# A fused attention and SwiGLU kernel on one core: one hand-kept order and engine table replaced by another

## The chip, the cores and the metric

The kernel runs on 1 core of one Trainium2 chip. The metric is the device time of one execution in microseconds (us). The kernel before took 261.92 us (median of 3 runs, 260.77 to 262.48). The engines of the core are TensorE (PE), VectorE (DVE), ScalarE (ACT), GpSimd (POOL) and SyncE (SP), which issues nearly all transfers.

## The reference

Attention over 4 batches, 8 heads, 768 positions of 64 values, then a feed-forward block on the 3072 tokens of 512 values:

```python
scores = q @ k.T / sqrt(64)
# heads 0, 2, 6: causal; the other heads: causal, and only the first 4 keys or the last 64
a = softmax(where(mask, scores, -1e9));  x = (a @ v) -> [3072, 512]
g = x @ w_gate                           # 512 -> 1536
out = (g * sigmoid(g) * (x @ w_val)) @ w_out   # 1536 -> 512
```

All inputs and outputs are float32. The kernel computes in float16 with float32 accumulation.

## The kernel before

The kernel first describes its work as 1073 named steps. Each has the engines that may run it, in a fixed order. Two long strings then decide everything that matters here. `ORDER` lists the steps, two characters each in base 62, in the order in which they are emitted, so it is each engine's order too. `WAYS` holds one digit per step and picks its engine. Numbers from 3700 up in `ORDER` are fillers: that many matmuls of the identity, whose result nobody reads.

```python
class Plan:
    FILL = 3700
    def order(self):
        n = len(self.tasks)
        numbers = [DIGITS.index(ORDER[2*i]) * 62 + DIGITS.index(ORDER[2*i+1])
                   for i in range(len(ORDER) // 2)]
        ...                             # a check of both strings, cut
        for t, w in zip(self.tasks, WAYS):
            t.way = t.ways[int(w)]          # engine of this step
        return numbers
...
for number in P.order():
    if number < P.FILL: P.tasks[number].run()
    else:               warm(number - P.FILL)   # fillers

def copy(task, dst, src):                        # all casts, copies, evictions (L175, L177)
    if task.way == "ACT": nc.scalar.copy(out=dst, in_=src)
    else:                 ENG[task.way].tensor_copy(out=dst, in_=src)
```

The steps with a choice that the argument touches are these (cut):

```python
P.add(f"cx{n}.{m}.{j}", ["ACT","DVE","POOL"], castv ...)      # V block n, float32 to float16, into vt
P.add(f"wc {kd}{n}",    ["ACT","DVE","POOL"], wcast ...)      # weights: g gate, v value, o output
P.add(f"mask{t}.{u}",   ["DVE","POOL"],       mask ...)       # L557: e = e * m, both in SBUF
P.add(f"sk{b}.{i}", ["DVE","POOL","ACT"], sinks_k ...)        # copies of the first 4 keys
P.add(f"sv{b}.{i}", ["DVE","POOL","ACT"], sinks_v ...)        # and of their values, inside SBUF
P.add("fill3",          ["DVE","POOL"],       ...)            # zero fill of hqz
P.add(f"oe{g}.{tt}",    ["ACT","DVE"],        ...)            # eviction of an output tile, from PSUM
# only DVE:  stt1: sil = (tanh + 1) * gate      stt2: h = sil * 0.5 * value     (L780, L787)
#            rc, nm: the division after attention (L574, L586)
```

The chain of a token tile runs like this. Load (SP), cast, transpose (PE), eviction to kT/qT, scores (PE, L539), exp (ACT, L549), mask (L557), attention times values (PE, L569), division (DVE, L586), transpose (PE, L602), gate and value matmuls (PE, L770), tanh (ACT, L776), stt1 and stt2 (DVE), output matmuls (PE, L799), eviction and store. Each engine runs its steps in the order of its list, so a late step delays those behind it: in the kernel before, VectorE's mask of 61.66 us took 1.79 us, and the multiply for h behind it started at 63.38 us.

The softmax here doesn't subtract the row's maximum and nothing guards it: scores larger than these inputs give would overflow.

## Time and profile before

| | before |
|---|---|
| median time | 261.92 us |
| profiled span | 259.0 us |
| useful TensorE work (own count over the matmul records) | 235.0 us |
| fillers | 131 matmuls, 40 of them in the opening block |
| DVE / ACT / POOL busy | 178.5 / 134.1 / 86.2 us |
| granted TensorE clock | 1.00 from 5.49 us until after the last matmul |

How to read it: TensorE is the bound, and "useful" is what it cannot do without. I give every useful matmul the distance to the next one that it shows when packed back to back; the prediction lists these distances, and the two matmuls of 384 columns get 162 ns. In a stretch of the timeline, what remains after the useful work is **lost**: fillers, or waits. All comparisons below are made in lost microseconds per stretch. The profile lines of this kernel that carry the argument stand in the prediction.

### The profile page before, as it was taken

To read this page: it belongs to the slowest core of one execution; us is meant where nothing else is said; L and a number is where in the kernel's file an instruction comes from. 1 tells how busy PE (TensorE), PEld (TensorE's weight loads), DVE (VectorE), ACT (ScalarE), POOL (GpSimd) and SP (SyncE) were. 2 spreads that over 40 slices of the span, in tenths; PEclk is the share of its full clock that TensorE was granted. 3 is DMA by queue.
4 is the path that set the end of the run, shared out by engine and by line. 5 is a ranking of instruction groups with operands and counts; after the bars stand their busy time and mean duration, and the time that the engine had idled before them with its cause. 6 is when DMAs were issued, how large, how long until landed. Compare 5 with 4: busy or idle time off the path is not lost.

```text
span 259.0 us, 5044 instructions
## 1 busy us (share of the span) xinstructions
PE 248.4 (96%) x1910; PEld 142.9 (55%) x1910; DVE 178.5 (69%) x360; ACT 134.1 (52%) x210; POOL 86.2 (33%) x122
## 2 busy tenths in 40 slices
PE   7979999998998999999999999999999999999992
PEld 7967667664554645555555546555545544444440
DVE  2877999989877676684877698776656547354621
ACT  2568977776764546596565445434752403421000
POOL 7335997672352355504802652000330000000000
PEclk9999999999999999999999999999999999999999
DMA  7999999966985799999569875551012320111243
GB/s 189 292 305 316 337 314 315 337 164 158 345 246 114 194 202 231 318 223 220 113 122 240 168 138 126 104 122 23 0 41 63 67 55 3 41 39 43 53 114 81
DMA packets 80377, 42.55 MB, mean 164 GB/s; under 512 B 32736, under 2 KB 75744, under 8 KB 80352
## 3 DMA queue, kind: packets, MB, share of 16 engines
q1 hardware_dynamic: 80272, 42.09, 66.8%
q8 instruction: 15, 0.25, 0.4%
q10 hardware_dynamic: 80, 0.13, 0.2%
q14 instruction: 10, 0.08, 0.1%
HBM read 28.31 MB, written 6.29 MB: 134 GB/s over the span
## 4 chain that ended last, share of the span: by engine, by line
PE 82%; DMA 6%; DVE 5%; SPq 3%; issue 1%; ACT 1%; POOL 0%; DVEq 0%; POOLq 0%; ACTq 0%
PE gv L770 43%; PE o_ps L799 23%; PE sc L539 8%; PE av L569 5%; DMA raw<-in_q_dram 3%; SPq L309 2%; DMA raw<-in_k_dram 2%; DVE h L787 1%; DVE vt L177 1%; PE xtr L602 1%; ACT e L549 1%; DVE sil L780 1%; DVE e L557 1%; DVE xb L586 1%; PE warm L285 1%
## 5 line engine op out<-in xcount | busy, mean ns | idle before, releaser
L549 ACT ACTIVATE e<-sc 128x1024 f16<-128x1024 f32 (+4 forms) x71 | 62.1, 878 | 32.4 <-PE sc L539 31.8
L770 PE MATMUL gv<-xt,wg_sb 128*128 128x512 f16 (+1 forms) x304 | 72.7, 368 | 1.6 <-DVE h L787 1.5
L770 PE MATMUL gv<-xt,wv_sb 128*128 128x512 f16 (+1 forms) x304 | 72.3, 368 | 0.6 <-DVE sil L780 0.6
L799 PE MATMUL o_ps<-wo_sb,h 128*128 128x512 f16 x288 | 69.4, 379 | 0.0
L776 ACT ACTIVATE sig<-gv 128x512 f32<-128x512 f32 (+1 forms) x76 | 43.1, 575 | 43.8 <-PE gv L770 42.1
L780 DVE SCALAR_TENSOR_TENSOR sil<-sig,gv 128x512 f32<-128x512 f32 (+1 forms) x76 | 49.1, 654 | 21.3 <-ACT sig L776 19.9
L787 DVE SCALAR_TENSOR_TENSOR h<-sil,gv 128x512 f16<-128x512 f32 (+1 forms) x76 | 49.2, 655 | 18.8 <-PE gv L770 17.3
L770 PEld LDWEIGHTS <-wv_sb 128*128 128x128 f16 x304 | 28.9, 98 | 28.4 <-issue 1.0
L799 PEld LDWEIGHTS <-h 128*128 128x128 f16 x288 | 27.6, 98 | 30.2
L770 PEld LDWEIGHTS <-wg_sb 128*128 128x128 f16 x304 | 28.6, 98 | 28.3 <-issue 2.1
L539 PE MATMUL sc<-qT,kT 128*128 128x256 f16 (+1 forms) x276 | 37.4, 257 | 0.2 <-ACT e L549 0.2
L557 POOL TENSOR_TENSOR e<-e,m 128x1024 f16<-128x1024 f16 (+1 forms) x15 | 28.5, 1903 | 23.7 <-ACT e L549 18.2
L539 PEld LDWEIGHTS <-kT 128*128 128x128 f16 x276 | 24.5, 97 | 11.0 <-issue 0.6
L569 PEld LDWEIGHTS <-e 128*128 128x128 f16 x472 | 19.9, 97 | 8.6 <-DVE xb L586 1.3
L569 PE MATMUL av<-vt,e 128*128 128x65 f16 x472 | 22.0, 193 | 1.0 <-DVE xb L586 0.7
L175 ACT COPY o_sb<-o_ps 128x512 f32<-128x512 f32 x13 | 7.6, 584 | 29.0 <-PE o_ps L799 27.9
L586 DVE TENSOR_TENSOR xb<-av,rc 128x256 f16<-128x256 f32 x47 | 19.8, 424 | 1.6
L177 POOL CAST hq<-raw 128x1024 f16<-128x1024 f32 (+1 forms) x12 | 12.0, 1001 | 17.9 <-DMA raw<-in_k_dram 12.1
L557 DVE TENSOR_TENSOR e<-e,m 128x640 f16<-128x640 f16 (+1 forms) x23 | 15.2, 667 | 2.7 <-ACT e L549 2.6
L177 POOL CAST vt<-raw 64x512 f16<-64x512 f32 x22 | 15.4, 700 | 5.0 <-DMA raw<-in_v_dram 3.4
L177 POOL COPY vt<-vt 2x330 f16<-2x330 f16 x18 | 8.4, 464 | 22.9 <-PE av L569 22.4
L574 DVE RECIPROCAL rc<-av 128x4 f32<-128x4 f32 x48 | 8.4, 176 | 9.9 <-PE av L569 9.7
(61 smaller groups left out, 142.2 us busy)
## 6 DMA issues: line engine op xcount, KB each, us to landing
raw<-in_q_dram SPq DMA_DIRECT2D x12, 512.0 KB, 5.5
raw<-in_k_dram SPq DMA_DIRECT2D x12, 512.0 KB, 6.7
raw<-in_v_dram SPq DMA_DIRECT2D x12, 512.0 KB, 6.5
out_dram<-o_sb SPq DMA_DIRECT2D x47, 128.0 KB, 2.4
raw<-in_moe_w_gate_dram SPq DMA_DIRECT2D x6, 512.0 KB, 7.1
raw<-in_moe_w_val_dram SPq DMA_DIRECT2D x6, 512.0 KB, 7.7
raw<-in_moe_w_out_dram SPq DMA_DIRECT2D x6, 512.0 KB, 6.7
xt<-xb SPq DMA_TRANSPOSE x16, 2.5
```

The source lines that it names most:

```text
L177: ENG[task.way].tensor_copy(out=dst, in_=src)
L539: nc.tensor.matmul(sc[c // 4][:, c % 4:c % 4 + n, :], weights, moving, start=first, stop=last)
L549: nc.scalar.activation(out=e[:, 0:n], in_=whole_sc.pop((t, u))[:, 0:n], func=AF.Exp, scale=scale)
L557: ENG[task().way].tensor_tensor(out=ev, in0=ev, in1=mm, op=ALU.mult)
L569: nc.tensor.matmul(av[:, n, 0:65], ee, vv, start=(m == 0), stop=(m == len(bl) - 1))
L574: nc.vector.reciprocal(out=rc, in_=avs[t, odd][:, :, 64:65])
L586: nc.vector.tensor_tensor(out=xbs[t][:, :, odd, :], in0=av[:, :, 0:64], in1=rc.to_broadcast([128, 4, 64]), op=ALU.mult)
L770: nc.tensor.matmul(ps, wsb[:, kk, j * 128:(j + 1) * 128], xt[:, kk, c[0]:c[1]], start=(kk == 0), stop=(kk == 3))
L776: nc.scalar.activation(out=sg[g, j, c], in_=gs[g, j, c], func=AF.Tanh, scale=0.5)
L780: nc.vector.scalar_tensor_tensor(out=sl[g, j, c], in0=sg.pop((g, j, c)), scalar=1.0, op0=ALU.add, in1=gs.pop((g, j, c)), op1=ALU.mult)
L787: nc.vector.scalar_tensor_tensor(out=hs[g, j][:, c[0]:c[1]], in0=sl.pop((g, j, c)), scalar=0.5, op0=ALU.mult, in1=vs.pop((g, j, c)), op1=A ...
L799: nc.tensor.matmul(o_open[g, tt], hs[g, j][:, tt * 128:(tt + 1) * 128], wo_sb[:, j, :], start=(j == 0), stop=(j == NJ - 1))
```

## The change

The intent: keep VectorE's copies, casts and masks, whose operands lie in SBUF, apart in time from GpSimd's work, since such a step beside GpSimd's took up to 1.79 us instead of 0.67 (lines in the prediction); reorder the loads for the start; drop fillers. Nothing but the two strings changes. All 35 lines of them differ, so the diff is cut to its head.

```diff
 ORDER = (
-    "030208041L0900011Mxr1T0B1X1N1W1O1V1Uxz1Y1Z1axw1n0C2526281o0A1r1d1K1P2D272H1e1t1u2E1p0E0D2I2G2K2J"
 ...
+    "0004081L021M1T1U09011W1N1Oxy1Y1V1a1Z1Xxr1t1u031r1s0B0A25262D2G1P2H1R1S2F1p1b1d1c1Q1n1f1y1z1e0C27"
 ...
 WAYS = (
-    "000000000000000000000000000000000000000000000000000000000000002222222222022200211200210211100111"
+    "000000000000000000000000000000000000000000000000000000000000002100222222022020222210101220101110"
 ...
```

Decoded, by kind of step (before to after). In all, 115 steps change their engine; kinds whose counts change by one at most (casts and evictions of Q and K, evictions to the gate's input) are left out.

| kind | DVE | POOL | ACT |
|---|---|---|---|
| masks | 23 to 20 | 15 to 18 | |
| key sink copies (steps) | 4 to 1 | 8 to 11 | |
| value sink copies (steps) | 5 to 3 | | 2 to 4 |
| casts of V | 14 to 11 | | 12 to 15 |
| value weight casts | 1 to 0 | 5 to 4 | 1 to 3 |
| gate weight casts | | 5 to 6 | 1 to 0 |
| output weight casts | | 5 to 4 | 1 to 2 |
| output evictions | 10 to 15 | | 14 to 9 |
| zero fill of hqz | 1 to 0 | 0 to 1 | |

Loads, with x for V, g, v, o for weights, in order of issue:

```
before: q0 k0 q1 k1 x0 q2 x1 k2 g1 v1 q3 g2 k3 x2 v2 g0 g4 v0 ...
after:  q0 k0 q1 x0 k1 q2 k2 x1 g1 v1 g0 q3 x2 k3 g2 v0 g4 v2 ...
```

Fillers after the opening block of 40: 91 become 50 (18, 11, 11, 5 and 5).

More of the change, by code (lines that the diff above doesn't have):

```diff
@@ L16 @@
 ORDER = (
-    "030208041L0900011Mxr1T0B1X1N1W1O1V1Uxz1Y1Z1axw1n0C2526281o0A1r1d1K1P2D272H1e1t1u2E1p0E0D2I2G2K2J"
-    "1b2F1c0F1q1Qxv1f1s1R1S1g2V2j2W0j1i211h1j0p1v1w1x1y2C1k2p2q0H2r2A2k1z2Lxw1l2M1m292N2O2X15202P2s2B"
-    "2t2Z2axm232b162Y2x2y0k2c249Z2d2e2h2i2Q2u2v0I9j2R362S2T2U9k3Q9lxo309o9a319b053W2g9p073X9m9n9q180G"
-    "3D3E3Y06229y9z3R3A9r3B9s3Z9c3M3a2w9d9t0q9u9eA02l2z2m32333b0i199f9g2o9w0m9v343c3G9x35A1A2109F3H9h"
-    "1E9i3C9G112n370o3e9K0l129H0K9L3p13389M9P9Q9I3I9S9J3f9U9R3d0J3j3k9V3FAI9W9T3t3u391B0L3T493U9N9X3J"
@@ L22 @@
-    "4F3K3w9Y2fA80n4H9OAD3S4GAJAK3L3x1H3hA9AE3NAF4A4I3i3lAN3z3V3vAS0s1FAAAL3m3g3n404JAM3o413OAGAOAPAT"
-    "420O3q3y43440t4N4q4O1IA3453PAH4K3r464LAV0M3sAU47A44WAWA54Z0r0u4a1C48AB4CA6A7AC4M4f0N4BBLAQ0v4o4y"
-    "4g4c4xARBMBN4S4T4b4p4EBOBP4dBaBb4v4wBf4l4QBQBc0QBgBh4PBRB6Bd0PBS4D4eB7Be4RB152530z0w4UB24X0x5WB8"
-    "B94VBA4rBBBC4zB3504hBT17B45556BU1J545DBD4YBiBE0RB55G4iBj5H5I0y1D4s0U1ABG4j4k4nBk4m5V5cBF14BHAX5d"
-    "AY5MAw4tBI1G4uAZ5N5X5eAz5O5fAa5P51595AAcBl570SAdAeAb585B5EAxAyB0Af5C5JAr0b5K5L5Q5RBn63Bm6B5b5g5S"
@@ L27 @@
-    "5h5TAhAiBV5ZBoBWAsAt5FAj5iAk5r0TBXBY5Y5s5j5k5UAmBJBKAn5o625a615p0XD2D35lAoAl6A5q68BZApC969D4Au5m"
-    "CACE5tAv7S5uBpBqCJ5vCBCH6i5yCFCG0V677RCI6I665wCiCK6J0WCj0h65CMCL5z6F6G7TCNAq6g6HBr0a6qCC0YCD8b6C"
-    "Cl6h64CkCm6DCnCoBsAgCpCq5n6pCr6OCY6E7PCZ6X6YCaCsCtD0Bu6R6S6TCx6oCy8d5xCzD1Bv6UBw6n6VCd6K0ZCb6L6l"
-    "6d6r7XBx6M6PCe0g6sCuByCTCU6NBzCc6u6Q6ZCf6v6W7OC0C1606a7N7VD5D66b6k6e7Q6zBt6c7W70CO6jC2Cv6xC46w6f"
-    "Cw756yC57U0d8c6m788e79CVC6CWC7C87v7B6t71CPCQ7C0f72Dy83DvDwCX730c7Y7ZDxDzE5CRCg7GE6E77HCSE0Ch7gE8"
@@ L32 @@
-    "D774E1E27h76E9EKEL7a7ED87tEM7bDR7ADS7FDUD9Dl7c7uDTDm7dDVDA7j7kDnDoDpE37iDb0e7e7mE47DDcDd7zDq81Dg"
-    "Dh7q7l7nDi8a7w8280848Z8i85DCC3Dr7o7r777pDjDk8788DD7I7JDsDEDF7KDB7L897f7x8Y8f8G8MDWDHDt8g8NDX868C"
-    "DuDY8AEAEN8BEB8P7MEFEO8hEG8QDZDI8D8EECDa8J8KEHDJDK7sEIEJ8HEDDe8FEoEEF3DfEpEq8VDMDN7yFXFYEr8O8L8R"
-    "8S8m8nDOF48TFZ8j8kEsF5FDFEFFFaFbDG8UDL8x8IEt8l938WEuFGEvFI8t94FH8r8sFcFdDPFeDQ9091EwEPEQExFJFK8p"
-    "8qFfEj8uERFgFNESEkF6F7ETEUEV8o8v988w8zFOFP92ElFLEWEXFSFQFTFM958y99FU9AEy9BEYFR96EzF1EZ8XF0979CF2"
@@ L37 @@
-    "F89D9EEaEbEcF9FAFVFBEmFWEeEfEgEnEhFCG6GkG7G8GlG9GmGAGnEdGLGMGoGpGNGsFhGQFiFjGqGrGtGRGSFkGOGPGGGH"
-    "GuGvGwFlGaFmGJGIGKGbGxFnFoFpGcGdGeG1FrFqGTG2GyFsFtGfGgG3GBFuGhGUFwFxGCGVGDGEGFG4G5FvGWFyGYGiFzG0"
-    "GXGZGjEiGzH0H1H4H5H6H9H2HAHBH3H7H8HEHFHGHCHDHHHI"
+    "0004081L021M1T1U09011W1N1Oxy1Y1V1a1Z1Xxr1t1u031r1s0B0A25262D2G1P2H1R1S2F1p1b1d1c1Q1n1f1y1z1e0C27"
+    "282I1o2E1q1g2K2Jxr2V0E2j1h0F211i1v1w1x2p2r2q2W2L222k2M1jxl2s200D2t2X1k2C292A2N1l2O2P2B1mxl2Z0j15"
+    "230p2Y2u242v2a2b162c9Z9a2d2e1K9j0i9k0H2Q2R2S2h9m0G2i0I9b2x0k36112T3Q0o9l9n9c9d2U9o052y2f9e9f3W06"
@@ new lines @@
+    "109p3X0m3A9g9q3B9h9P2m9i9Q9r30319F3Y9G3R2l9s2n3D183Z3E9y072z133G3H2w32129R9S9H3a9t3M3j3k9T331E9u"
+    "0q199I9J349v3h9z3CAD3iAE35AF0n371HA1A03b3F2o3c0J3S380L3I3J0K3V9wA23T9K9x9L9M393e9X3K9UAS3L3O3f9V"
+    "0t9W3p9N0s493P3N0l9Y0r3t3d4A9O3u4I0x3gATANAO1I2g3U3l3z4JAP1B0NAI404FAUAQ3mAVAR3n4H0M3vAW3o1C1F3w"
+    "4G3qA3AJAK3xAG3y434E3r0OA44142A84N3s444OAH4546A6A94K4LA5A74C47480vAL0R4B1D0zAMAB4W174c4dAAArAsAC"
+    "0u4MAu0yBVAt4Z4SBWAvBXAw4P4aBYBZ0w4QAzBf4q4R4TAxAy4l4f0V4o4p4w4UBiB0BgBh1ABkBjBn4V4X14BlBm4gAXBa"
@@ new lines @@
+    "1J4bBoB64D4h4yB7B84xBb5XBcBT1GAYAZAa4vBQ5253Ac0Q4eAd544zBLBRBSBUBd504Y4iBe55BGAe51Af5D565W5J5K0P"
+    "0SAbBHBI4uB14j4k5V5G5HAhAi0e4t5L66575Z584r4sAj4m5MB259B95ABM675IBNBA0UAkAm5B5c5C5d5N5EBB63B3B45Q"
+    "5RAg5O5fAn5P5S7z5e5TAoB50TAl5g5b624nAp5hBOBEBp5oBCBD5F5aBP5p5Y5UBJCYCZBF0X5rCsBKCT61645i696BCa0W"
+    "6i5j5k5sCUBqBrCVCt6A685lCv7xCuCwCOCP5mBsCR5q5uCQ5vCJ0YCW6h5y6FCKAqCS6GCXCLCxCyCzCb0aCc5t5w5z6g6q"
+    "6CD06OCq6D6IBu6J6oCnCo6U6H0b6VD1Ci0ZCj6jCpCr656pCk5xBv6n6E6R6S7NC9CABwCgBtCB6X6T6W6K5n606kClCC6L"
@@ new lines @@
+    "6Y7P7X6d6M6r6P7RCmBxByCD6NCdCe0hBzC06Z6Q0d6s6uD26v6aCf7O6b6c757vCE6e6wCF6fChCG7E7FC1CM6t6z0c7W7T"
+    "D3C2CHCIC470C5716xD46m6yCN7VE5E6E8C6E7787U797SE9D5D6Dq7A8372EA0g7BEBDrECEKDsC77C73Db7Q74ELDcDd7j"
+    "7k8bDt7lD7C8Du6l7Y7ZDW7D76EMENEODv7t7aDX7I7JDZ0fDYDa7G7H7uD8EFDwDx7g7K7LD9DADy8aDzED7b7c80DlDC7d"
+    "7hEEDm7y7qEG81827eDn8h8YC3Dg7i8iDBDDDE777f8ZEH87DF88EIEJDhDUDi848G857mDRDoDpDS8e8ADH7nDIDTDV7w8B"
+    "7MDJ8P8Q7oDeE08JDK8K8g7pDfDMDN89867r8CDGE18M8D8N7sFXE2FYE3E4FZEtEuDODP8f8V8jEv8k8E8F8L8HFaEwFbDj"
@@ L40 @@
+    "8pExFI8qDkEP8RDQ8cEQER8OFN8SFOFPFJ8m8xFQFK8T8WFD8n90FRFEFFFS8U91Ej8oESDLEkEmElEUEn8d938l8t8uFGEo"
+    "EV94Ep8I8rFHEqFTFUFVEW8s8v8yEX8wEY92F8FWErF98X8zFLFM9A9BEZFAEa95EbEsEcFc96F3Fd97Ff98EeET99Fe9CFg"
+    "9DFBFCEyEfEgF6F4EzF0F1F5EhF79EG6F2G7GpGqG8GBGsGCGrGtGDFhGEGfG1EiGgGFGhG2FiFjFkFlGLG4FmG3GQEdG5GM"
+    "GNGRGiGjGGGHFnFoFpFqGTFrFsFtGSGUGIGOGkGVGPGlFuFwGYGWGXGZG9FxGAGnGmGoGJGKFyFvGaGbFzG0GdGuGvGcGeGw"
+    "GxGzH0GyH1H2H3H4H5H6H7H8H9HAHBHCHEHDHFHGHHHI"
 )
 WAYS = (
-    "000000000000000000000000000000000000000000000000000000000000002222222222022200211200210211100111"
@@ L43 @@
-    "011000000000101000000000000000100211222010101101100000000000000000000110121220201101000000000000"
-    "100000100000000011012220220000000000000000000010000100100000000002220000110100000000000011000000"
-    "100000010002212020000000000000000002100000000000000001012121000000100000001001000001001200220000"
-    "000000000000210001001000000220020202200000000010000000020000100000000000012022110000001000000010"
-    "000000110122120100000000000000001000000000000000201020111000000100000000000100001000000000000000"
@@ L48 @@
-    "000000000000000000000000000000000000000000000000000000000000000000000000000000000000000000000000"
-    "000000000000000000000000000000000000000000000000000000000000000000000000001000000000000000000000"
-    "000000000000000000000000000000000000000000000000100001000010000100000000000000000000000000000000"
-    "000000000000000000000000000000000000000000100000000000000000000000000000000000000000000000000000"
-    "000000000000000000000000001000010000000000000000000000000000000000000000000000000000000000000000"
@@ L53 @@
-    "10000000001000000"
+    "000000000000000000000000000000000000000000000000000000000000002100222222022020222210101220101110"
+    "011000000100000000000000000001201112020210011101100000000010000000000110022022001101000001000000"
+    "110000000100000011002220220010100000000000000200000000100000000000222020000100000000000011000000"
+    "100000011000212000000001001000000002000010000000000002010202000000100000001001000021021102220000"
+    "000000000000110000000000000020022111000000000010000000012000000000000000021011200000000000000000"
@@ new lines @@
+    "000000200102221200000010010000001100010000000001102201100000000100100000000120001001000000000000"
+    "000000000000000000000000000000000000000000000000000000000000000000000000000000000000010000000001"
+    "000000000000000000000000000000000000000000000000000000000000000010000100001000010000000000000000"
+    "000000000000000000000000000000000000000000000000000001000010000100000000000000000000000000000000"
+    "000000000000000000000000000000000000000000100001000000000000000000000000000000000000000000000000"
@@ L54 @@
+    "000000000000000000000000001000000000000000000000000000000000000000000000000000000000000000000000"
+    "10000100001000000"
 )
```

## The prediction

> **What bounds the kernel now.** I began with the page's span, the busy time of each engine and the 40 slices.
>
> ```profile
> span 259.0 us, 5044 instructions
> PE 248.4 (96%) x1910; PEld 142.9 (55%) x1910; DVE 178.5 (69%) x360; ACT 134.1 (52%) x210; POOL 86.2 (33%) x122
> PE   7979999998998999999999999999999999999992
> DVE  2877999989877676684877698776656547354621
> POOL 7335997672352355504802652000330000000000
> ```
>
> TensorE (PE) is full nearly everywhere, VectorE (DVE) is close to full only from the fifth to the thirteenth slice, GpSimd (POOL) matters in the first half alone. But "96% busy" counts fillers (matmuls of the identity that are thrown away) and counts overlapping matmuls as one stretch, so it doesn't say how much could be won. For that I took the start of each of the 1910 matmul records in the trace and the distance to the next start. Back to back, that distance is 216 ns for 512 columns, 109 for 256, 56 for 128 and 30 for the 65-column ones. Counting each useful matmul at its own figure gives 62.3 us for the output projection (288 matmuls), 124.3 for gate and value (608), 28.1 for scores and masks, 13.9 for attention times values, 6.2 for transposes and 0.2 for the mask order: **235.0 us of useful TensorE work**. It is the same before and after. The first useful matmul starts at 6.17 us, the last one at 253.9 us. In between are 247.7 us, so 12.7 us are lost, and 5.1 us follow for the last eviction and store. That 12.7 us is all there is to win after the first data; a perfect order would end near 246.3 us.
>
> Then the same stretch by stretch, with the view of windows.
>
> ```profile
> 6.17:22.50 16.33, 14.95 (x228) 13.29 (x226) 13.57 (x36) 10.15 (x19) 6.47 (x8) 1.00 1.15 303
> 22.50:60.00 37.50, 36.42 (x371) 25.64 (x368) 33.98 (x80) 31.21 (x47) 28.94 (x42) 1.00 0.99 283
> 60.00:90.00 30.00, 28.44 (x232) 15.75 (x231) 23.91 (x44) 17.90 (x29) 11.06 (x14) 1.00 0.84 222
> 90.00:160.00 70.00, 69.57 (x483) 37.10 (x480) 51.61 (x98) 41.84 (x67) 30.49 (x34) 1.00 0.92 195
> 160.00:254.00 94.00, 94.00 (x567) 46.33 (x563) 52.78 (x99) 30.49 (x49) 4.55 (x4) 1.00 0.25 55
> ```
>
> The columns are the stretch, its length, then busy us and count of PE, its weight load, DVE, ACT, POOL, then clock, DMA share and GB/s. Useful work by my count is 9.8 us of the first stretch, 34.6 of the second, about 28.2, 68.7 and 93.7 of the others. So the losses are **6.5, 2.9, 1.8, 1.3 and 0.2 us**. In the first stretch 72 fillers (4.0 us at 56 ns) stand in for waiting; there the DMA queues are full (share 1.15) and work can only start as loads land. From 160 us on nothing can be won.
>
> Last, the timeline at the largest single gaps. Two of them:
>
> ```profile
> 61.51 1.39 POOL L557 TENSOR_TENSOR e<-e,m 128x640 f16<-128x640 f16 x1 [1.28 <-ACT e L549]
> 61.66 1.79 DVE L557 TENSOR_TENSOR e<-e,m 128x1024 f16<-128x1024 f16 x1
> 64.10 1.24 PE L770 MATMUL gv<-xt,wg_sb 128*128 128x512 f16 x5 [0.80 <-DVE h L787]
> ...
> 77.48 1.26 DVE L177 COPY vt<-vt 2x330 f16<-2x330 f16 x2
> 77.60 1.04 POOL L177 CAST wo_sb<-raw 128x1024 f16<-128x1024 f32 x1 [2.95 <-DMA raw<-in_moe_w_out_dram]
> 78.70 0.61 POOL L177 CAST vt<-raw 64x512 f16<-64x512 f32 x1
> 78.77 0.83 DVE L177 CAST hqz<-raw 128x512 f16<-128x512 f32 x1
> 80.24 1.02 PE L770 MATMUL gv<-xt,wg_sb 128*128 128x512 f16 x4 [0.70 <-DVE h L787]
> ```
>
> The columns are start, duration, engine, line, what. A mask multiply of this size takes 0.67 us on DVE when alone; here it starts just behind one of POOL's and takes 1.79, the multiply for h that stands behind it is late, the PSUM buffer isn't freed, and TensorE loses 0.96 us. At 77 to 80 us the same happens with a copy (0.23 us at its fastest, 1.02 for the first here) and a cast (0.42, here 0.83): 0.87 us lost. Around 37 us a pair of the same copies beside POOL's weight casts costs 0.92 us more. These three make 2.7 us on the path.
>
> [...] the copies from PSUM lie within a few per cent of their mean (0.688 us for an output tile). Comparing every DVE instruction with the shortest of its own form, I get 15.6 us of excess, some 11 of it in SBUF copies, casts and masks, and 4.0 on POOL. [...] The trace shows matmuls 107 ns apart until 5.4 us and 56 after that, and a granted clock of 1.00 throughout; the longest gap is 1 us, so 41 fillers fewer should cost no clock.
>
> **The change, part by part.** I decoded both orders into their named steps.
>
> 1. Fillers: 131 become 90 (40 in the opening block, then 18, 11, 11, 5, 5). Removing 41 at 56 ns is 2.3 us of TensorE time, but they stand in waits. On the path I count only the opening: 51 fillers hold TensorE to 6.17 us though the cast of the first load ends at 5.7; 0.4 us, which the next wait for a load takes back.
>
> 2. Loads. The second V block comes before the second K, the third K before the second V, the gate weights of columns 0 to 255 move from 16th to 11th, the sixth K from 25th to 30th. Loads land about 1.7 us apart. The first gate matmul stands at 22.50 us, behind transposes of the third K (20.16), which needs a load that lands near 18.9. One place earlier it lands near 17.1, POOL casts it by 18.2 (1.04 us), and the transposes can run then. Following the new order from there with the trace's durations (exp 1.02, casts of V 0.62, PE groups 0.24 to 0.45), the limit becomes the cast of the gate weights, which land at 20.28, so the first gate matmul can start near 21.4: **1.1 us won** of the 6.5. The rest of that stretch waits for loads 3 to 8, whose total doesn't change.
>
> 3. 22.5 to 60 us: weights earlier, value matmuls within 1.5 us of their gates (in the kernel before the first value group comes at 26.7), no fillers. Of 2.9 us lost, 0.92 is the contention at 37, 0.45 fillers. I expect **1.2 won**.
>
> 4. DVE and POOL. DVE instructions [...] fall from 67 to 49 (casts of V 14 to 11, sink copies 18 to 8 instructions, masks 23 to 20, weight casts 2 to 1, other casts 10 to 9). By the rows of the profile: sink copies of V 4 x 0.57, of K 3 x 0.41, casts of V 3 x 0.56, masks 13 x 0.57 + 10 x 0.79 becoming 8 and 12 (1.3 us), zero fill 0.9, weight 0.7, small ones 0.4, together 8.5 us off; five more output evictions (5 x 0.69), and others 0.4 on: DVE's own work falls by 4.7 us, and by 8 before 80 us, where it was over 85% busy. If half of the 11 us of excess goes too, DVE's busy time ends near 168 us. POOL gains 3 masks, 3 sink copies, and the 2 us zero fill. On the path: the two gaps shown (1.8 us) should go, but new order makes new meetings; I give **1.2** for 60 to 90 us and **0.6** for 90 to 160.
>
> 5. The end: the last 48 output matmuls, eviction and store stand in the same order: 0.
>
> Sum: 1.1 + 1.2 + 1.2 + 0.6 = 4.1 us. 261.9 - 4.1 = **257.8 us**, 1.6% faster.
>
> **Rivals.**
> POOL becomes the bound. Between the third load's casts and the last mask before 50 us its list adds up to 26.7 us (15 casts at 1.04, V casts at 0.6, masks at 1.40, copies) from about 19.5, so it has no slack until 46 us[...]. For it: POOL was 97% busy from 30 to 40 us before and didn't hold TensorE. Against: three weight casts go to ACT. It would eat steps 3 and 4: about 260.5.
> Loads bound the first 50 us anyway. For: the queue share is over 1.1 there. Then step 2 and half of 3 are worth nothing, and the time is about 259.5.
> All waits of DVE go. [...] 60 to 160 us lose nothing (3.1 us won) and 22.5 to 60 only the 0.5 for loads (2.4): 255.3 with the start.
>
> **Range and chances.** Three runs of the kernel before spread over 1.7 us, so noise is small beside these. The rivals span 255.3 to 260.5; I take 254.6 to 260.8. Faster by over 2% means under 256.7, 1.1 us below my figure: it needs most of rival three, 0.35. Slower by over 2% would need 5 us of new waits where nothing was added, 0.03. Within 2%: 0.62.
>
> **What would show it.** Right: DVE's busy time near 168 us; hardly a DVE mask, cast or SBUF copy over 1.5 times its shortest; first gate matmul near 21.4 us; no TensorE gap of 0.8 us after 60 us; matmuls still 56 ns apart for 128 columns after 6 us. Wrong: first gate matmul at 22.5 or later (step 2), long POOL waits ahead of gate matmuls at 25 to 50 us (rival one), gaps of 0.5 us or more past 90 us, or a clock below 1 in a slice.

## The result

The changed kernel takes **258.52 us** (median of 4 runs, 257.98 to 258.92) against 261.35 us of the kernel before in the same rounds (4 runs, 260.47 to 262.48). Ratios here and below are the mean time of one kernel's fast runs over that of the other's fast runs of the same rounds, so they are not quite the ratio of the medians. This one is 0.9888, with a 95% interval of 0.9841 to 0.9935. That is 1.1% faster, and inside the 2% that counts as the same. It was predicted at 257.8 us, from 254.6 to 260.8.

The page of the changed kernel, for its span, its engines and the slices of DVE:

```profile
span 256.6 us, 4959 instructions
PE 246.3 (96%) x1869; PEld 140.3 (55%) x1869; DVE 169.2 (66%) x347; ACT 136.0 (53%) x215; POOL 89.8 (35%) x130
DVE  3757999987944676759756968648465566436431
```

DVE's busy time fell by 9.3 us. It is as full as before from the fifth to the eighth slice; slices 12 and 13 (71 to 83 us) fell from seven tenths to four. TensorE's "96%" stands unmoved, and so says nothing. The windows do, in the same columns as in the prediction:

```profile
6.17:22.50 16.33, 13.66 (x190) 11.13 (x187) 11.04 (x30) 11.72 (x22) 7.03 (x11) 1.00 1.17 307
22.50:60.00 37.50, 36.58 (x367) 25.23 (x368) 33.83 (x79) 31.48 (x49) 29.28 (x40) 1.00 1.10 327
60.00:90.00 30.00, 30.00 (x219) 16.36 (x218) 19.50 (x39) 19.07 (x31) 15.58 (x18) 1.00 0.90 200
```

From 60 to 90 us TensorE is busy for all 30.00 us where it was for 28.44. DVE does 4.4 us less there, and POOL 4.5 us more. In the first stretch TensorE is busy 1.3 us less than before, since fillers are gone. This does not yet say whether useful work came earlier. My own count over the matmul records does:

| stretch, us | lost before | lost after | change |
|---|---|---|---|
| 0 to 6.17 | 6.17 | 5.75 | -0.42 |
| 6.17 to 22.5 | 6.58 | 7.22 | +0.64 |
| 22.5 to 40 | 2.71 | 2.18 | -0.53 |
| 40 to 60 | 0.30 | 0.10 | -0.20 |
| 60 to 90 | 2.16 | 0.07 | -2.09 |
| 90 to 160 | 1.14 | 0.92 | -0.22 |
| 160 to the last matmul | 0.17 | 0.09 | -0.08 |
| sum | 19.23 | 16.33 | -2.90 |

The last matmul ends at 251.29 us instead of 254.11, and the eviction and store after it take 5.3 us instead of 4.9. Three quarters of the gain lie between 60 and 90 us, and the start gave nothing. Differences of a few tenths must be read with care, since each is between two single traces. The run e1 below has the order, loads and fillers of the kernel before, and yet it starts useful work at 5.67 us. Between 90 and 160 us, where e1 and e4 have the steps of the kernel before, they lose 0.4 and 0.75 us more than it.

The DVE steps that took longer beside GpSimd's, in the view of groups of one form each (line, engine, operation, operands, count, then busy us and mean ns). First the kernel before:

```profile
L177 DVE CAST hqz<-raw 128x512 f16<-128x512 f32 x5 | 4.8, 955 | 1.8 <-DMA raw<-in_q_dram 1.7
L177 DVE COPY vt<-vt 2x330 f16<-2x330 f16 x10 | 5.7, 571 | 0.1
```

Then the same two forms in the changed kernel:

```profile
L177 DVE COPY vt<-vt 2x330 f16<-2x330 f16 x6 | 1.4, 234 | 0.1
L177 DVE CAST hqz<-raw 128x512 f16<-128x512 f32 x3 | 1.3, 420 | 0.0
```

The same instruction takes 234 instead of 571 ns and 420 instead of 955 ns. Nothing in it was changed; it stands elsewhere. Over all DVE steps whose operands lie in SBUF alone, the excess over the shortest of the same form fell from 11.3 us in 67 instructions to 3.5 us in 49. Those that took over 1.5 times their shortest fell from 13 to 4.

How this looks in the timeline (start, duration, engine, line, what), in the changed kernel near the place of the second gap that the prediction shows:

```profile
78.36 2.13 POOL L557 TENSOR_TENSOR e<-e,m 128x1024 f16<-128x1024 f16 x1 [0.77 <-ACT e L549]
78.98 0.69 DVE L787 SCALAR_TENSOR_TENSOR h<-sil,gv 128x512 f16<-128x512 f32 x1 [0.32 <-PE gv L770]
```

GpSimd holds a mask for 2.13 us, and DVE in that time does a step that reads one operand from PSUM. It takes 0.69 us, and all 68 steps of this form take 0.67 to 0.69. TensorE has no gap over 0.35 us after 60 us.

One collision is left on the path, at 31 to 33 us:

```profile
31.39 1.40 POOL L557 TENSOR_TENSOR e<-e,m 128x640 f16<-128x640 f16 x1
31.96 1.37 DVE L557 TENSOR_TENSOR e<-e,m 128x1024 f16<-128x1024 f16 x1
33.39 0.42 PE L569 MATMUL av<-vt,e 128*128 128x65 f16 x8 [0.36 <-DVE e L557]
```

DVE's mask starts 0.57 us behind GpSimd's and takes 1.37 instead of 0.67 us. TensorE's attention matmuls wait for it.

Last the start. The third K's transposes and the first gate matmul in the kernel before:

```profile
20.16 0.61 PE L427 MATMUL tr<-ident,hq 128*128 128x128 f16 x8
...
22.50 0.60 PE L770 MATMUL gv<-xt,wg_sb 128*128 128x256 f16 x4
```

And in the changed kernel:

```profile
18.31 0.62 PE L427 MATMUL tr<-ident,hq 128*128 128x128 f16 x8 [0.66 <-POOL hq L177]
...
18.97 0.69 DVE L177 COPY kT<-tr 128x1024 f16<-128x1024 f16 x1 [0.87 <-PE tr L427]
18.99 1.28 POOL L177 CAST vt<-raw 64x512 f16<-64x512 f32 x2 [0.74 <-DMA raw<-in_v_dram]
...
19.57 0.41 DVE L586 TENSOR_TENSOR xb<-av,rc 128x256 f16<-128x256 f32 x1
20.02 0.53 DVE L177 CAST vt<-raw 64x512 f16<-64x512 f32 x1
...
20.80 0.42 DVE L586 TENSOR_TENSOR xb<-av,rc 128x256 f16<-128x256 f32 x1
...
21.37 0.40 PE L569 MATMUL av<-vt,e 128*128 128x65 f16 x8 [0.65 <-DVE xb L586]
...
22.76 1.04 PE L770 MATMUL gv<-xt,wg_sb 128*128 128x256 f16 x8
```

The transposes did come 1.85 us earlier, but the first gate matmul came 0.26 us later: 4.45 us pass between the two instead of 2.34. The attention matmuls at 21.37 us stand before the gate, and they wait for DVE. DVE's list there is, in order, the eviction of the third K (18.97), a division (19.57), a cast of V (20.02) and the next division (20.80). The V block, which had to give way to the K, landed later; in the kernel before, DVE had cast it at 17.13 us, ahead of all this. The other casts of V (18.99 to 20.27 us on POOL) do not bind: in the run e6 they end at 20.33 us, and the gate starts at 22.14.

### The profile page after: what moved, and what is told of

The parts are those of the page before. It is cut to its first block, busy times and chain, and to the rows that moved or that the text cites. A ratio compares the mean times of both kernels' runs of the same rounds, so it can differ in the third digit from the quotient of the medians.

```text
span 256.6 us, 4959 instructions
## 1 busy us (share of the span) xinstructions
PE 246.3 (96%) x1869; PEld 140.3 (55%) x1869; DVE 169.2 (66%) x347; ACT 136.0 (53%) x215; POOL 89.8 (35%) x130
## 4 chain that ended last, share of the span: by engine, by line
PE 82%; DMA 5%; SPq 5%; DVE 4%; issue 1%; POOL 1%; ACT 0%; POOLq 0%; DVEq 0%; ACTq 0%
PE gv L770 45%; PE o_ps L799 23%; PE sc L539 8%; PE av L569 5%; SPq L309 3%; DMA raw<-in_k_dram 3%; DMA qT<-hqz 2%; SPq L414 1%; DVE m L248 1%; PE xtr L602 1%; DVE vt L177 1%; DVE e L557 1%; DVE xb L586 0%; DVE h L787 0%; PE tr L427 0%
## 5 line engine op out<-in xcount | busy, mean ns | idle before, releaser
L549 ACT ACTIVATE e<-sc 128x1024 f16<-128x1024 f32 (+4 forms) x71 | 62.2, 879 | 38.9 <-PE sc L539 38.2
L787 DVE SCALAR_TENSOR_TENSOR h<-sil,gv 128x512 f16<-128x512 f32 (+1 forms) x76 | 49.6, 656 | 22.5 <-PE gv L770 20.5
L557 POOL TENSOR_TENSOR e<-e,m 128x640 f16<-128x640 f16 (+1 forms) x18 | 31.4, 1750 | 9.4 <-ACT e L549 9.2
L177 POOL CAST vt<-raw 64x512 f16<-64x512 f32 x22 | 13.4, 614 | 12.5 <-DMA raw<-in_v_dram 6.1
L177 DVE COPY o_sb<-o_ps 128x512 f32<-128x512 f32 x15 | 10.3, 687 | 7.7 <-PE o_ps L799 7.7
L557 DVE TENSOR_TENSOR e<-e,m 128x1024 f16<-128x1024 f16 (+1 forms) x20 | 14.5, 728 | 0.0
L177 POOL CAST hq<-raw 128x1024 f16<-128x1024 f32 (+1 forms) x9 | 9.0, 999 | 15.1 <-DMA raw<-in_k_dram 9.9
L177 POOL CAST hqz<-raw 128x512 f16<-128x512 f32 x6 | 3.9, 658 | 28.8 <-DVE xb L586 18.8
```

What stands on the lines that cost most here:

```text
L549: nc.scalar.activation(out=e[:, 0:n], in_=whole_sc.pop((t, u))[:, 0:n], func=AF.Exp, scale=scale)
L557: ENG[task().way].tensor_tensor(out=ev, in0=ev, in1=mm, op=ALU.mult)
L787: nc.vector.scalar_tensor_tensor(out=hs[g, j][:, c[0]:c[1]], in0=sl.pop((g, j, c)), scalar=0.5, op0=ALU.mult, in1=vs.pop((g, j, c)), op1=A ...
```

## The experiments

Twelve kernels ran, and one more did not build. The theory was the prediction's: the loss after 60 us comes from DVE steps on SBUF operands that stand beside POOL's (1.79 us instead of 0.67), and the start is set by loads. The rivals were that the new order or the fillers did it, or that chains of casts and waits, and not the loads, set the start.

### e1: three steps of the kernel before moved to another engine

```diff
 # kernel before, WAYS only (3 digits)
- mask9.1: POOL    sv1.3: DVE    sv0.2: DVE
+ mask9.1: DVE     sv1.3: ACT    sv0.2: ACT
```

> The kernel before with three small steps put on other engines: the mask multiply that POOL ran from 61.51 us goes to VectorE, and the two sink copies of V that VectorE ran at 36.7 and 77.5 us go to ScalarE. Order, loads and fillers stay. Theory 1 [...]: the three gaps of TensorE at 37, 63 and 79 us (0.92, 0.96 and 0.87 us) shrink to under 0.3 us each and the time falls by 1.8 to 2.7 us, to 258.7 to 259.5 beside a kernel before of 261.3. Theory 2 (the waits are given back by the next narrow place, so an engine choice alone is worth little): under 0.7 us faster.

Measured: 258.97 us (258.68 to 259.42), the kernel before 260.48 on the same chip; ratio 0.9935 (0.9918 to 0.9953), which is 1.7 us, just short of the 1.8 to 2.7 expected. The stretch from 60 to 90 us lost 0.33 us instead of 2.16. The timeline of e1 at the gap of 61 us:

```profile
61.79 0.68 DVE L557 TENSOR_TENSOR e<-e,m 128x1024 f16<-128x1024 f16 x1
62.39 0.68 DVE L787 SCALAR_TENSOR_TENSOR h<-sil,gv 128x512 f16<-128x512 f32 x1
```

With GpSimd's mask away from beside it, the same mask takes 0.68 instead of 1.79 us, and the h step behind it is no longer late. So 1.83 us of the gain between 60 and 90 us come from the engines alone: the order is the old one, and all fillers are there. The third move won nothing. The gap at 37 us only shifted: there are now two waits, of 0.30 us from 38.2 and of 0.66 us from 38.7 us.

### e2 and e3: one string without the other

```diff
 # e2
  ORDER of the kernel before
- WAYS of the kernel before
+ WAYS of the changed kernel
 # e3: ORDER of the changed kernel, WAYS of the kernel before
```

> The order, loads and fillers of the kernel before with the engine of every step as in the changed kernel. Theory 1a (moving copies off VectorE is enough by itself): VectorE's busy time falls to about 170 us and the time by 2 us or more. Theory 1b (a step meets GpSimd by where it stands, so engines without the order only change which ones meet): VectorE's excess over the shortest of each form stays at 6 us or more in SBUF-only steps, and the time lies between 0.8 us faster and 2 us slower than before.

> The new order, loads and fillers with the engine of every step as in the kernel before. If loads, order and fillers are the gain, it keeps 2 us or more of the 2.8. [...] VectorE's excess in SBUF-only steps goes back from 3.5 us to 8 us or more, TensorE's waits between 40 and 160 us from 1.1 us to 2.5 us or more, and the gain shrinks to under 1 us, or turns into a loss.

Measured: e2 took 286.54 us (ratio 1.0991) and e3 276.79 us (ratio 1.0625). Both are far slower than either kernel, and outside what any theory had allowed. I had thought of the two strings as two parts whose worths add up. The traces show why they don't. In e2, POOL and then TensorE:

```profile
87.94 2.13 POOL L557 TENSOR_TENSOR e<-e,m 128x1024 f16<-128x1024 f16 x1 [3.33 <-ACT e L549]
...
92.73 2.02 POOL L177 CAST wo_sb<-raw 128x1024 f16<-128x1024 f32 x2
93.82 1.44 PE L799 MATMUL o_ps<-wo_sb,h 128*128 128x512 f16 x3 [4.87 <-POOL wo_sb L177]
```

The output matmuls need these weight casts. In POOL's list the casts stand behind a mask that had to wait 3.33 us for its exp, and behind a cast and copies. TensorE stands idle for 4.87 us until the first of the two is done. Its granted clock is then halved from 92.44 to 99.27 us, as it is from 51.48 to 54.90. In e3 the same happens on ACT:

```profile
88.94 0.59 ACT L175 COPY o_sb<-o_ps 128x512 f32<-128x512 f32 x1 [2.87 <-PE o_ps L799]
...
90.80 0.60 PE L539 MATMUL sc<-qT,kT 128*128 128x256 f16 x5 [1.90 <-ACT e L549]
```

An eviction given to ACT waits 2.87 us for output matmuls, the exp behind it waits too, and TensorE waits 1.90 us for the exp. In these two runs an engine table is good only with the order that it was made for. Their times therefore say nothing on how much of the gain belongs to order and how much to engines. The excess of DVE's SBUF-only steps over the shortest of their form does say something: about 6.6 us in e2 and 6.3 us in e3, against 11.3 and 3.5 in the two kernels. Each string alone takes away some 5 of the 8 us, though in schedules that long waits have pulled apart. For e2 that is what was expected (6 or more), for e3 less than its second case (8 or more), in which the meetings of DVE with GpSimd are the gain.

### e4 and e6: the fillers

```diff
 # e4: kernel before, the seven later filler entries
- 11 19 16 15 16 6 8
+  0 18 11 11  5 5 0
 # e6: changed kernel, the five later filler entries dropped
- 18 11 11 5 5
```

> The kernel before with 41 fillers fewer, cut to the counts of the changed kernel (40, then 0, 18, 11, 11, 5, 5, 0). Theory: fillers stand in waits, so the time moves by less than 0.4 us (0.3 at most from the opening) and TensorE's waits grow by about what the fillers took. Rival a (fillers are on the path): 1.5 to 2.3 us faster. Rival b (they keep the clock up): matmuls of 128 columns 107 ns apart again after 6 us, and over 0.8 us slower.

> The changed kernel without its 50 fillers after the opening 40. Theory: they only stand in waits, time within 0.3 us of the changed kernel, TensorE's waits before 22.5 us rise by about the 2.8 us that the fillers took. Rival: the clock falls (128-column matmuls 107 ns apart after 6 us), and the time rises by 0.5 us or more.

Measured: e4 took 260.88 us, ratio 1.0014 (0.9998 to 1.0031). e6 took 258.90 us, ratio 0.9932 (0.9906 to 0.9959). That interval overlaps the changed kernel's (0.9841 to 0.9935), and the medians are 0.4 us apart. In the trace of e6 the stretch from 6.17 to 22.5 us loses 6.66 us, all of it waits, so most of the fillers stood in waits. That it is 0.56 us less than the 7.22 of the changed kernel is not the fillers' doing:

```profile
15.78 1.04 POOL L177 CAST hq<-raw 128x1024 f16<-128x1024 f32 x1 [0.40 <-DMA raw<-in_k_dram]
...
17.73 0.61 PE L427 MATMUL tr<-ident,hq 128*128 128x128 f16 x8 [0.50 <-DVE rc L574]
...
22.14 1.04 PE L770 MATMUL gv<-xt,wg_sb 128*128 128x256 f16 x8
```

In this execution the third K had landed by 15.78 us, and in the changed kernel its cast waited for the load until 17.22, although the loads are the same. Transposes and gate then come 0.6 us earlier together, as they would if DVE's list between them set the distance.

The matmuls stay 56 ns apart. One of e6's seven runs took 260.24 us and had the lowest mean clock of them, 0.992; the others had 0.995 to 1.000. (A mean of 0.996 needs no slow stretch: the profiled run of the changed kernel has it, and its clock falls only after the last matmul, at 254.60 us.) So the fillers cost nothing measurable, and dropping 41 of them won nothing. Whether the last 50 are a safeguard for some executions stays open.

### e5: the one collision left on the path

```diff
 # changed kernel, WAYS only
- mask4.1: POOL
+ mask4.1: DVE
```

> The changed kernel with one of its masks of 640 columns, which POOL starts at 31.39 us just ahead of a VectorE mask, put on VectorE too. [...] the VectorE mask of 1024 columns falls from 1.37 to about 0.68 us, TensorE's wait of 0.52 us at 33 us goes, and 0.2 to 0.5 us of the time with it, if the waits of 22 to 40 us aren't filled by a load. Rival: this stretch is bound by loads, so under 0.15 us.

Measured: 258.18 us, the kernel before 260.75; ratio 0.9910 (0.9892 to 0.9928). The wait at 33 us fell from 0.52 us (distance between matmuls over the packed one) to 0.22, and the stretch from 22.5 to 40 us lost 1.83 us instead of 2.18. The time is not measurably better than the changed kernel's: a third of a microsecond is as large as the spread of its runs.

### e7 and e9: the second V before the third K again

The old order of these two loads, inside the new order:

```diff
 # changed kernel, ORDER only
- ... load q2, load k2, load x1 ...
+ ... load q2, load x1, load k2 ...
 # e9 also on POOL: the casts of V block 1 ahead of the cast of the third K
```

> The changed kernel with the third K and the second V loaded in the old order (V first), and GpSimd's casts of them in that order too. My prediction had put 1.1 us on this swap. Theory now (the wait only moved from K to V, because both are needed before the first gate matmul): first gate matmul within 0.6 us of 22.8, time within 0.5 us of the changed kernel. Rival (the prediction's step): 0.8 us or more slower than the changed kernel.

e7 did not build, because the load then stood behind a step that uses it in the emitted order. e9 is the mended form.

> The changed kernel with the third K and the second V loaded in the old order (V first), and GpSimd's casts of them in that order too (the build that failed, mended). My prediction had put 1.1 us on this swap. Theory now (the wait only moved from K to V, because both are needed before the first gate matmul): first gate matmul within 0.6 us of 22.8, time within 0.5 us of the changed kernel. Rival (the prediction's step): 0.8 us or more slower than the changed kernel.

Measured: 262.98 us median of 20 runs, from 260.80 to 266.98. The kernel before took 261.04; ratio 1.0065 (1.0042 to 1.0088) over the 15 runs that count as fast, which is 4.6 us slower than the changed kernel by the two ratios. In the profiled run (260.84 us):

```profile
19.88 0.62 PE L427 MATMUL tr<-ident,hq 128*128 128x128 f16 x8 [2.35 <-POOL hq L177]
...
24.16 1.04 PE L770 MATMUL gv<-xt,wg_sb 128*128 128x256 f16 x8
```

The third K's transposes come 1.57 us later than in the changed kernel, and the first gate matmul 1.40 us later. My theory had been that the wait only moves from K to V and that the swap is worth nothing. It falls. Inside the new order the swap is worth about 1.4 us at the first gate matmul.

The scatter of 6 us goes with the clock. Over the 20 runs the mean granted clock lies between 0.975 and 0.997, and its correlation with the span is -0.87. The fastest run has 0.997; the five over 265.8 us have 0.975 to 0.987. The profiled run had one of the high clocks, so no trace here shows where the clock was lost in the slow ones. e8 shows such a place.

### e8 and e10: two loads left out, and one cast moved

Wrong results on purpose: the second K and the second V are not loaded, and their casts read the first blocks. All later loads come about two places earlier.

```diff
 # e8: changed kernel, in load()
+ if n == 1 and kind in "kx":
+     landed[kind, 1] = landed[kind, 0]
+     return
 # e10: as e8, and one cast of V block 1
- cx1.1.1: DVE
+ cx1.1.1: ACT, right behind cx1.0.1
```

> The changed kernel without the loads of the second K and the second V; the casts read the first K and V in their place, so the result is wrong on purpose and every instruction of the compute engines stays. Theory (the first 22.5 us wait for loads as a whole): the first gate matmul moves from 22.8 to 19.5 to 20.5 us and the time falls by 2 to 3 us. Rival (the start is bound by the chain of casts, exps and evictions): the gate moves by under 1 us and the time by under 0.7 us.

> As the run with two loads less (wrong result on purpose), but the V cast that VectorE waited 2.3 us for GpSimd to begin there is on ScalarE. [...] that wait of TensorE (2.8 us at 20 us) goes, and the time falls by 2.5 us or more against the run with two loads less. Loads theory (the first 22.5 us wait for loads): then the first gate matmul comes at 19.5 to 21 us and the time is 1.5 us or more below the changed kernel. Rival (chains of casts, exps and evictions bind the start): the gate at 21.5 us or later and the time within 1 us of the changed kernel.

Measured: e8 took 261.84 us (259.82 to 263.10), ratio 1.0035 (1.0009 to 1.0060): over 3 us **slower** than the changed kernel (3.3 by the medians, 3.8 by the ratios), with 1 MB less to load. The first gate matmul came at 24.86 us, 2.1 us later, so neither expectation came true. e10 took 259.11 us (258.39 to 259.67), ratio 0.9919 (0.9888 to 0.9949). The one cast was worth 2.7 us in the medians, and 3.0 us by the ratios (0.0116 of 261 us). In the timeline of e8:

```profile
18.86 1.04 POOL L177 CAST wv_sb<-raw 128x1024 f16<-128x1024 f32 x1
19.25 2.67 DVE L177 CAST vt<-raw 64x512 f16<-64x512 f32 x1
...
19.84 1.81 POOL L408 MEMSET hqz<- 128x2048 f16 x1
...
22.74 0.60 PE L572 MATMUL av<-vt,e 128*128 128x65 f16 x8 [2.79 <-DVE xb L589]
```

With loads out of the way, POOL's work stands back to back. DVE's cast of V (0.41 us alone) begins 0.39 us behind POOL's cast and ends at 21.92 us, 0.27 us after the end of the fill that follows on POOL. By these spans it was held up by two instructions in a row, not by one. The division behind it is late, and TensorE stands still for 2.8 us. The windows around the end of this wait show a second cost:

```profile
19.27:22.68 3.41, 0.68 (x9) 0.50 (x9) 3.34 (x4) 0.66 (x1) 2.37 (x2) 1.00 1.08 264
22.68:26.09 3.41, 3.35 (x30) 2.76 (x31) 1.46 (x5) 1.75 (x3) 0.19 (x1) 0.50 0.91 283
```

The column ahead of the last two is the granted clock: 1.00, then 0.50. The halved clock lasts from 22.68 to 26.09 us. That is 3.41 us at half speed, at most 1.7 us of lost work. TensorE's idle time ahead of it was 2.80 us, from the last filler's end to the next matmul, and in the 3.41 us ahead of the fall TensorE was busy for 0.68 us.

The clock records show when the other changes came. In the kernel before the clock rose at 5.49 us and fell 252.59 us later; in the changed kernel it rose at 5.43 and fell 249.17 us later; in e2 the two falls lie 40.96 us apart. These are 74, 73 and 12 times 3.413 us, and the halved stretches last once (3.41 us in e8, 3.42 in e2) or twice as long (6.83 in e2). The length of a wait alone did not decide in these traces: in e2 the fall at 51.48 us follows a wait of 1.95 us (1.46 us of matmuls in the 3.41 us ahead of it), while a wait of 2.18 us, from 16.47 us in the same trace, and the 2.35 us in the profiled run of e9 left the clock at 1.00. What does decide is not shown, and so it is not shown either why e9's times scatter with the clock; no trace of one of its slow runs was kept.

All eight runs of e8 have a mean clock of 0.988 to 0.995, lower than those of the changed kernel (0.996 to 0.999).

e10, with the cast on ACT:

```profile
18.24 1.26 ACT L175 CAST vt<-raw 64x512 f16<-64x512 f32 x2
...
21.59 1.04 PE L773 MATMUL gv<-xt,wg_sb 128*128 128x256 f16 x8
```

The first gate matmul now comes at 21.59 us, 1.17 us earlier than in the changed kernel, and the clock is 1.00 in its trace. Still the time is no better than the changed kernel's: the stretch from 22.5 to 40 us lost 3.43 us instead of 2.18. So the loads alone do not bound the start; of the three expectations, the loads' failed; the first (TensorE's wait of 2.8 us goes, 2.5 us or more won against e8) and that of the chains held. What comes earlier runs into the next chain of casts and masks, and into a new collision:

```profile
30.91 1.03 POOL L177 CAST wg_sb<-raw 128x1024 f16<-128x1024 f32 x1
...
31.34 2.12 DVE L560 TENSOR_TENSOR e<-e,m 128x1024 f16<-128x1024 f16 x1
31.89 1.03 POOL L177 CAST wv_sb<-raw 128x1024 f16<-128x1024 f32 x1
...
33.52 0.42 PE L572 MATMUL av<-vt,e 128*128 128x65 f16 x8 [0.97 <-DVE e L560]
```

Again DVE's step (0.67 us alone) ends only after a second GpSimd instruction has ended, here 0.54 us after it. The spans on GpSimd are rough, and e8 and e10 give one observation each.

### e11 to e13: trying to win the start

```diff
 # e11: changed kernel
+ a division (nm0.0) ahead of an eviction (evk2.0)
- cx1.1.1: DVE, mask4.1: POOL
+ cx1.1.1: ACT, mask4.1: DVE
+ the second half of the mask fill later; the last two filler entries (5, 5) dropped
 # e12: as e11
+ the first half of the mask fill later too, one Q eviction (evq3.10) earlier
 # e13: changed kernel, nm0.0, cx1.1.1, mask4.1 and fillers as e11, mask fill where it was
+ two casts of V behind a gate weight cast on POOL; the third V's load behind that of g2
```

> The changed kernel with six small edits for its start: one division by the sum moved ahead of an eviction on VectorE, the V cast of 20.0 us to ScalarE, one mask from GpSimd to VectorE, the second mask fill (first used long after) behind 50 us, the two groups of 5 fillers dropped. If the waits at 20.5 us (0.8) and 33 us (0.5) are chains and not loads, first gate matmul near 21.8 us and 1.0 to 1.8 us faster than the changed kernel. If loads bind this stretch, under 0.4 us.

> As the tuned kernel a, and on VectorE the first mask fill (1.6 us) stands behind two gate multiplies and an eviction instead of ahead of them. If the wait of 0.44 us at 28.3 us is VectorE's order, 0.3 to 0.8 us faster than tuned a; if the masks then come late, within 0.3 us of it.

> The changed kernel with the start of the tuned kernels (one division earlier, the V cast of 20.0 us on ScalarE, one mask on VectorE, two groups of fillers dropped), the mask fill left in its old place, and the gate weights whose cast TensorE waited for at 31 us loaded and cast one place earlier, ahead of the third V. If those weights' load was what gave the gain of the tuned kernels back, TensorE's wait at 31 us stays under 0.4 us, and the time is 0.7 to 1.3 us below the changed kernel, a ratio to the kernel before of 0.984 to 0.986. If any earlier step is just met by the next load, under 0.3 us.

Measured: e11 258.76 us (ratio 0.9904), e12 258.46 us (0.9896), e13 257.77 us (257.60 to 258.07; 0.9890, 0.9868 to 0.9911). In e11 the first gate matmul came at 21.93 us, 0.8 us earlier, and it was given back at 31 us:

```profile
30.81 1.38 POOL L177 CAST wg_sb<-raw 128x1024 f16<-128x1024 f32 x1
...
32.25 1.04 PE L770 MATMUL gv<-xt,wg_sb 128*128 128x512 f16 x4 [1.25 <-POOL wg_sb L177]
```

A cast of gate weights on POOL (1.04 us alone) stands beside two DVE masks there, takes 1.38 us, and TensorE waits for it. In e12 that wait is 0.81 us. e11 and e12 also lose 0.7 us at 59 us, where the moved half of the mask fill (1.41 us) stands on DVE ahead of a gate multiply. In e13, where the fill stands in its old place, that wait is gone, and so is the one at 31 us, as expected. e13 has the best median of all, and its last matmul ends at 250.68 us instead of 251.29. But its ratio, expected at 0.984 to 0.986, is that of the changed kernel (0.9890 and 0.9888), so it is not shown to be faster. None of the three is.

## Why the prediction was right

The sum held: the matmuls end 2.8 us earlier of the 4.1 predicted, and the time, 258.5 against 257.8, lies within the range. Its terms held less well, and that they came to so near a sum is partly luck: the 1.1 us of step 2 did not come, and 60 to 90 us gave 0.9 us more than forecast. The range was also wide enough to hold all three rivals' times.

- **Fillers (step 1).** 0.4 us for the opening, taken back by the next wait: 0.42 us were won before 6.17 us, and 0.64 lost in the stretch after it. The numbers fit, but the fillers are not shown to be the reason. e1 keeps all 51 and starts useful work at 5.67 us. In its trace the clock rose at 4.21 us, in that of the kernel before only at 5.49, and until then the fillers come 107 ns apart instead of 56. e4 and e6 show that the fillers as a whole are neutral. That 41 fewer would cost no clock was my estimate from a longest gap of 1 us; e4's 20 runs have mean clocks of 0.995 to 1.000.
- **Loads (step 2).** This step failed at the point that it named as its own test: "the first gate matmul can start near 21.4". It started at 22.76, which the prediction had named as the sign of this step being wrong. The first half of its working held (the third K's transposes at 18.31 us, 18.2 predicted for the cast). What it left out is DVE's list: the cast of the V block that had given way now stands on DVE between the third K's eviction and a division that TensorE needs, and this chain became the limit, not the cast of the gate weights. From the third K's transposes to the gate it takes 4.45 us, where the prediction's 18.2 and 21.4 leave 3.2. With that cast on ScalarE and the division earlier, e11 needs 3.92 us and starts the gate at 21.93. Its wording slips too. The first V, not "the second V block", comes before the second K. The sign of the swap was right nonetheless: e9 loses 1.4 us at the first gate matmul without it. That the old order's casts and divisions were simply arranged as well for 22.5 us is argued, not shown.
- **22.5 to 60 us (step 3).** 0.73 us won of 1.2 predicted. One collision remains at 32 us; e5 removes most of it and wins 0.35 us in its stretch.
- **DVE beside POOL (step 4).** For 60 to 90 us the cause was right and the term too small: 2.09 us instead of 1.2, since hardly any new meetings came, where I had allowed for some, and since the loss there was 2.16 us by the later count, not 1.8. e1 shows it by moving three steps: 1.83 us there. For 90 to 160 us 0.22 instead of 0.6, which two single traces do not tell from nothing. DVE's busy time came out at 169.2 us (168 predicted), and no gap of 0.8 us is left after 60 us.
- **The end (step 5).** 0 predicted; the tail grew by 0.4 us. From the end of the matmuls to the landing of the last store it takes 3.89 us in both traces, so the step itself was right. What grew lies behind that landing; its cause stays open.
- **The rivals.** POOL did not become the bound after 22.5 us, though e11 shows that it stands ready to. "Loads bound the first 50 us anyway" came true for the first 22.5 us in its outcome but not in its reason: e10 has 1 MB less to load and is no faster. "All waits of DVE go" came true only between 60 and 90 us.

What stays open: why e9's clock falls in some executions and not in others, and how much of the gain belongs to the order, which the times of e2 and e3 could not tell.

## What to carry to other kernels

When an instruction on VectorE takes twice its shortest, look at what GpSimd does at its start. Moving such a step to ScalarE or to another moment was worth 2.7 us here for one cast (e10 against e8) and 1.83 us between 60 and 90 us for two steps of e1, where in-order work that TensorE waits for stood behind it; the third step of e1 won nothing. An order and an engine table belong together: here either whole one with the other's old partner cost 16 to 26 us, though three single engine choices (e1) could be changed alone. A load that comes earlier pushes another back (here the third K's transposes came 1.85 us earlier and the first gate matmul 0.26 us later), so follow both through their casts to the same matmul before counting a gain.
